# Slot scatters issued one by one, behind a unit's maxima and behind its norm

## The chip, the cores and the metric

The kernel runs on one core of a Trainium2 chip. The metric is the device time of one execution in microseconds (us). TensorE (PE in the rows, PEld for its weight loads), VectorE (DVE), ScalarE (ACT), GpSimd (POOL) and SyncE (SP) run their own instruction streams and meet at semaphores. A row that says "<-remote" tells of a wait whose releaser the profile cannot name.

## The reference

Pooled attention feeds a mixture of experts with one expert per token. Cut to what matters:

```python
k_p = k.reshape(B, H, S // 8, 8, D).mean(axis=3)          # B, H, S, D = 8, 8, 576, 64
v_p = v.reshape(B, H, S // 8, 8, D).mean(axis=3)
scores = q @ k_p^T / sqrt(D)
attn = exp(scores - max) / sum(exp(scores - max))
x = (attn @ v_p) as 4608 tokens of 512
e = argmax(x @ w_gate)                                     # 8 experts, hidden size 1024
pos = running count of e, token by token                   # dropped beyond capacity 1152
y = relu(x @ w1[e]) @ w2[e];  out = softmax(x @ w_gate)[e] * y
```

All numbers are float32; the products of the expert part are made of three products of a high and a low part each.

## The kernel before

**Two parts.** The attention part (from L388 on) makes the 4608 token rows, writes them to `xs` in HBM, and finds for each token its place in a table `slots` in HBM that is sorted by expert. The expert part (L1297 on) is a loop over items of up to 256 tokens of one expert; it gathers rows of `xs` by the table, makes the two products, and scatters rows to the output. Between them stands `prologue` (L1008), which reads the table back (L1041, L1042) after the last scatter into it and does the first item.

**Units.** The attention part walks over 36 units of 128 tokens (L707), in pairs of batches: four units of the even batch, a tail unit made of the last 64 tokens of both (`Unit.tail`, its matmuls work on 64 rows at a time), four units of the odd batch. The loop at L1148 is a software pipeline written out by hand: its turn n makes the scores of unit n (L499), their maxima (`softmax`, L506: `mx`) and the subtraction (L511), the exponential of unit n-1 (L514), and of unit n-2 the transposes of the probabilities (L523, copied by ScalarE at L524), the product with the values (`av`, L535: `pa`) and `norm` (L546 to L554: `rz` is the reciprocal of the sums, `xo` the result). The order in the loop is the order on each engine; nothing is moved by a scheduler.

**Queues of small work.** Work that is no part of a unit waits in lists: `rq` (routing, generators of small VectorE instructions), `gq` (GpSimd's sums of keys and values, later the splitting of expert weights), `aq`, `dq`, and `sq` (the slot scatters). `step(list, n)` at fixed places of the turn takes n pieces from a list and so fixes where they stand.

**Routing and slot scatters.** When the 9 (later 4, 2 and 3) logit groups of a batch pair are there, `route` (L586) works out on VectorE for each token its slot (`gix`, L684) and its gate weight (`pairs`, L688). Then it puts one scatter per group of 128 tokens into `sq` (L702), 27 for the first three pairs and 9 for the last. A scatter (L690) is two GpSimd instructions: a copy of one column into `apart`, which reads the tile that `pace` names, and the indirect DMA (L696) that writes 128 entries of 8 bytes to `slots`. `pace` is set in `softmax` to the unit's maxima (L508), so that the copy, and with it the scatter, waits until VectorE has made them. In the last two turns, where no unit is scored, `pace` is empty and a memset (L695) stands for the copy.

Before the change the scatters of a turn stand together at its end (L1228): two in a turn up to turn 25, four from turn 26. At turn 28 `start_ids` (L845) issues what is left in `sq` and then SP's load of the first slots (L848); the gather of their rows follows on GpSimd (L97) among pieces of `w1l` (L128), and its rows are transposed at turns 31 and 32 (L884). At turn 25 SP loads weights (L843), at turn 33 more of them (L124). ScalarE issues the writes of token rows to `xs` (L582).

Of the kernel before, what the change touches and what calls it, by code (L numbers as in the profile page):

```python
# [10 lines left out]
F32 = mybir.dt.float32  # L11
# [10 lines left out]
P = 128  # L22
# [9 lines left out]
def pooled_attn_top1_moe(ctx: ExitStack, tc: tile.TileContext, q, k, v, wg, w1, w2, cap, out):  # L32
# [8 lines left out]
    B, H, S, D = q.shape  # L41
# [126 lines left out]
    with ExitStack() as actx:  # L168
# [3 lines left out]
        sm = actx.enter_context(tc.tile_pool(name="sm", bufs=2))  # L172
# [188 lines left out]
        def tail_tile(b):  # L361
            return (b // 2) * NPB + (2 * NB if b < LAST - 1 else NB + 2)
# [112 lines left out]
        class Unit:  # L475
# [65 lines left out]
            def norm(self):  # L541

                b, t = self.b, self.t
                av = self.pa.rearrange("p (h x) -> p h x", x=XW)
                rz = sm.tile([P, H, 1], F32, name="rz", tag="rz")
                nc.vector.tensor_scalar_add(rz, av[:, :, XW - 1 : XW], POOL * 1e-9)  # L546
                nc.vector.reciprocal(rz, rz)
                i = 0 if self.tail else t % 2
                if i == 0:
                    self.xo = wk.tile([P, 1 if self.tail else 2, H, XW - 1], F32, name="xo", tag="xt" if self.tail else "xo", bufs=1 if self.tail else 3)  # L550
                    first[b, t] = self.xo
                else:
                    self.xo = first[b, t - 1]
                nc.vector.tensor_mul(self.xo[:, i], av[:, :, 0 : XW - 1], rz.to_broadcast([P, H, XW - 1]))  # L554
                if not self.tail and i == 0:
                    return
                bp = b // 2
                if bp not in lgs:
                    lgs[bp] = sm.tile([P, NPB, E], F32, name="lg", tag="lg")
                if self.tail:  # L560
                    t0 = tail_tile(b) - bp * NPB
                elif b == LAST:
                    t0 = NB + 3 * (t // 2)
                else:
                    t0 = (b % 2) * NB + t - 1
                nc.vector.tensor_reduce(out=lgs[bp][:, t0 : t0 + i + 1], in_=self.xo[:, :, :, D:].rearrange("p i h e -> p i e h"), axis=AX.X, op=ALU.add)
                if self.tail:
                    for u, bb in enumerate(self.bs):
                        rows_out.append((xs[bb * S + NB * P : (bb + 1) * S, :].rearrange("p (h d) -> p h d", d=D), self.xo[u * TAIL : (u + 1) * TAIL, 0, :, 0:D]))
                else:  # L570
                    if b == LAST:
                        r0 = b * S + P * (t - 1)
                        dst = xs[r0 : r0 + 2 * P, :].rearrange("(p j) d -> p j d", j=2)
                    else:
                        dst = xs[b * S : b * S + NB * P, :].rearrange("(p j) d -> p j d", j=NB)[:, t - 1 : t + 1]
                    rows_out.append((dst.rearrange("p j (h d) -> p (j h) d", d=D), self.xo.rearrange("p j h x -> p (j h) x")[:, :, 0:D]))
# [128 lines left out]
        pace = []  # L705
# [5 lines left out]
        rq, aq, dq, sq, gq, held, hold = [], [], [], [], [], [], [1]  # L711
# [32 lines left out]
        def step(q_, n=1):  # L744

            while q_ and n and not (q_ is rq and held):
                if callable(q_[0]):
                    q_.pop(0)()
                    n -= 1
                    continue  # L750
                made = next(q_[0], 0)
                if made == 0:
                    q_.pop(0)
                elif made is not held:
                    n -= 1
                elif hold:
                    held.append(1)
# [6 lines left out]
        with tc.manual_schedule():  # L764
# [20 lines left out]
            def ahead(b):  # L785

                if b + 1 < B:
                    load_q(b + 1)
                if b == LAST - 1:
                    dq.append(masks)  # L790

            nu = len(units)
# [3 lines left out]
            n_late = n_early + 6  # L796
# [39 lines left out]
            def start_early():  # L836

                drain(rq)
                e0 = nc.values_load(esi[0:1, 0:1], engines=(SP,), min_val=0, max_val=E - 1)
                early["e0"] = e0  # L840
                early["w1"] = [kv_tile()[:, 0:2].rearrange("p f x -> p (f x)") for _ in range(KD)]
                for c in range(KD):
                    nc.sync.dma_start(early["w1"][c], rows(w1f, e0 * DM + c * P, P))  # L843
# [12 lines left out]
            def start_weights():  # L856
                drain(gq)
                kvx.close()
                wb = ctx.enter_context(tc.tile_pool(name="wb", bufs=1, side="right", reuse_waits="tile"))
                wr[1] = wb.tile([P, KD, DF], F32, name="r1")  # L860
                wr[2] = wb.tile([P, KF, DM], F32, name="r2")
                wr["h"] = wb.tile([P, KF, DM], F32R, name="w2h")
                wr["l"] = wb.tile([P, KF, DM], F32R, name="w2l")
                load_w2(early["e0"])
# [5 lines left out]
            def split_next():  # L870
                for c in range(2):
                    for f in range(0, DM, 256):
                        gq.append(partial(w2_piece, c, slice(f, f + 256), nc.gpsimd))
# [274 lines left out]
            for n in range(nu + 2):  # L1148
                u = units[n] if n < nu else None
                if u is None:  # L1150
                    pace.clear()
                p = units[n - 2] if n > 1 else None
                nx = units[n + 1] if n + 1 < nu else None
                new = n and u and u.b != units[n - 1].b
                if new:
                    assert not aq
                    ahead(u.b)
                if n == nu:
                    hold.clear()
                if n == n_start:  # L1160
                    start_weights()
                if n == n_start + 2:
                    split_next()
                if n == n_early:
                    start_early()
                if n == n_early + 3:
                    start_ids()
                    split_early()
                if n == n_early + 4:
                    start_rows()  # L1170
                if u:
                    u.score(0)
                if p and n <= nu:
                    p.p_t(0)
                if 0 < n <= nu:
                    units[n - 1].exp()
                fed = n > NB and nx and values_at(n)
                if fed:
                    nx.q_part()
                spread(n)  # L1180
                if u:
                    u.score(1)
                    if n == 0:
                        keys_first(1, kfirst)
                    u.softmax()
                step(aq)
                if p and n <= nu:
                    p.p_t(1)
                if n == nu:
                    sums()  # L1190
                if nx and not fed:
                    nx.q_part()
                if held:
                    held.clear()
                    step(rq)
                turns(n)
                flush()
                step(aq)
                if n == nu:
                    hidden(0, [0])  # L1200
                    units[n - 1].p_t(0)
                    units[n - 1].p_t(1)
                    step(gq, 4)
                if p:
                    p.open()
                    p.av(0)
                    p.av(1)
                if n == nu:
                    hidden(0, [1])
                if n >= n_late:  # L1210
                    step(rq, 7 if n < nu else 9 if n == nu else 2)
                step(dq)
                if p:
                    p.norm()
                if n_early + 6 <= n < n_early + 8:
                    transposed(n - n_early - 6, early["x"])
                if n < nu:
                    step(rq, 4 if n <= nu // 2 else 8 if n < n_late else 4)
                elif n == nu:
                    step(rq, 3)  # L1220
                r = p and route_of(p)
                if r:
                    rq.append(r)
                    if p.b == early_b - 1:
                        rq.append(favourite())
                hooks(n)
                step(gq, 4 if n < nu - 1 else 0)
                step(sq, 2 if n < nu - 10 else 4)  # L1228
                step(aq)
            flush()  # L1230
            prologue()
# [137 lines left out]
```

## Time and profile before

| | |
|---|---|
| time, median of 3 runs | 661.72 us (657.91 to 663.55) |
| the profiled execution's own time | 656.15 us |
| its span, first to last instruction | 654.5 us |
| PE busy | 607.1 us (93%) |
| PEld busy | 539.8 us (82%) |
| DVE busy | 339.2 us (52%) |
| POOL busy | 317.9 us (49%) |
| ACT busy | 223.6 us (34%) |
| mean granted TensorE clock | 0.979 |

Busy times are shares of one profiled execution. Ends of matmuls are modelled, so a busy TensorE need not be at its peak. A wait's releaser is inferred from semaphore events. The time of a GpSimd DMA row is that of the issue on the engine, not of the data's way to HBM.

### The profile page before, as it was taken

Reading aid. Unit: us, or ns where it says so; the run is one execution under the profiler, and the core shown is the slowest. Engines: PE = TensorE matmul, PEld = TensorE weight load, DVE = VectorE, ACT = ScalarE, POOL = GpSimd, SP = SyncE. Lnnn points to the kernel's source line nnn. Section 1 sums busy time; section 2 is a strip of 40 time slices with the busy share of each in tenths; the row PEclk is TensorE's granted clock in tenths of the full one; section 3 lists DMA queues with packets and bytes.
Section 4 is the critical chain, followed back from the end, with each engine's and each line's share of the span. In section 5 each row is a group of like instructions: output and inputs, shape, how many; then the busy total and the mean of one; then the engine's idle time right before and its main releaser. Section 6 shows DMA issues by size and latency. Waiting matters only on the chain. (4 is left out here: it accounts for less than half of the span.)

```text
span 654.5 us, 13915 instructions
## 1 busy us (share of the span) xinstructions
PE 607.1 (93%) x3966; PEld 539.8 (82%) x3967; DVE 339.2 (52%) x740; ACT 223.6 (34%) x414; POOL 317.9 (49%) x537
## 2 busy tenths in 40 slices
PE   2899979989779799999999999999999999999994
PEld 2789869878668588898989899888998889989983
DVE  4777867868767812246728642235432565222222
ACT  2465444546424111135517521115211473112111
POOL 7399979247645334215745413414444155431344
PEclk9999989999979899999999999999999999999997
DMA  9999996584622271107845652102721091110111
GB/s 314 301 255 334 310 264 121 118 242 98 177 46 54 73 300 64 32 32 238 298 159 178 248 204 64 64 20 77 263 64 56 12 316 31 64 42 22 64 48 65
DMA packets 103712, 93.79 MB, mean 143 GB/s; under 512 B 82820, under 2 KB 82820, under 8 KB 103688
## 3 DMA queue, kind: packets, MB, share of 16 engines
q1 hardware_dynamic: 54520, 62.47, 30.1%
q0 software_dynamic: 11392, 21.57, 10.4%
q10 hardware_dynamic: 37776, 9.46, 6.5%
q8 instruction: 12, 0.20, 0.1%
q14 instruction: 12, 0.10, 0.1%
HBM read 132.96 MB, written 31.27 MB: 251 GB/s over the span
## 5 line engine op out<-in xcount | busy, mean ns | idle before, releaser
L1269 DVE SCALAR_TENSOR_TENSOR hl<-ph,hh 128x512 fp32r<-128x512 f32 x60 | 40.8, 690 | 108.9 <-ACT hh L1268 78.0
L1268 ACT ACTIVATE hh<-ph 128x512 fp32r<-128x512 f32 x60 | 35.9, 599 | 171.2 <-PE ph L152 168.3
L165 PE MATMUL y<-w2h,hh 128*128 128x512 f32 x280 | 78.1, 400 | 0.0
L152 PE MATMUL ph<-xh,w1h 128*128 128x256 f32 x480 | 76.5, 281 | 1.2 <-ACT xo L1084 0.9
L165 PE MATMUL y<-w2l,hh 128*128 128x512 f32 x280 | 76.6, 395 | 0.0
L152 PE MATMUL ph<-xl,w1h 128*128 128x256 f32 x480 | 76.2, 280 | 0.4 <-DVE w1l L128 0.3
L152 PE MATMUL ph<-xh,w1l 128*128 128x256 f32 x480 | 76.0, 280 | 0.0
L97 POOL DMA_INDIRECT xg<-xs,ix x42 | 44.2, 1053 | 58.9 <-PE y L165 52.2
L165 PE MATMUL y<-w2h,hl 128*128 128x512 f32 x280 | 71.0, 396 | 0.0
L152 PEld LDWEIGHTS ph<-xh,w1h 128*128 128x128 f32 x480 | 65.7, 188 | 4.5 <-issue 1.9
L152 PEld LDWEIGHTS ph<-xl,w1h 128*128 128x128 f32 x480 | 65.0, 188 | 0.7 <-issue 0.7
L152 PEld LDWEIGHTS ph<-xh,w1l 128*128 128x128 f32 x480 | 65.0, 188 | 0.0
L165 PEld LDWEIGHTS y<-w2h,hl 128*128 128x128 f32 x280 | 52.6, 188 | 12.7
L165 PEld LDWEIGHTS y<-w2l,hh 128*128 128x128 f32 x280 | 52.6, 188 | 12.6
L535 PE MATMUL pa<-vbd,pT 126*128 126x146 f32 (+5 forms) x400 | 60.6, 313 | 0.0
L535 PEld LDWEIGHTS pa<-vbd,pT 126*128 126x128 f32 (+1 forms) x400 | 56.4, 184 | 3.0 <-issue 0.7
L165 PEld LDWEIGHTS y<-w2h,hh 128*128 128x128 f32 x280 | 50.0, 188 | 9.4
L524 ACT COPY pT<-pp 126x384 f32<-126x384 f32 x72 | 30.3, 422 | 78.6 <-PE pp L523 56.7
L128 DVE TENSOR_TENSOR xl<-px,xh 128x512 fp32r<-128x512 f32 x40 | 25.7, 686 | 57.2 <-ACT xh L127 57.2
L102 POOL DMA_INDIRECT out_dram<-zrow,iz x40 | 46.8, 1171 | 16.3 <-issue 15.1
L499 PE MATMUL ps<-kbs,qT 128*128 128x144 f32 (+1 forms) x320 | 52.9, 308 | 1.8 <-ACT qT L490 1.8
L95 POOL TENSOR_TENSOR guard<-ix 128x4 int32<-128x4 int32 x21 | 5.1, 244 | 101.6 <-DVE ix L92 101.3
(261 smaller groups left out, 1035.6 us busy)
## 6 DMA issues: line engine op xcount, KB each, us to landing
r<-in_moe_w_dram SPq DMA_DIRECT2D x86, 1024.0 KB
raw<-in_k_dram SPq DMA_DIRECT2D x12, 768.0 KB
raw<-in_v_dram SPq DMA_DIRECT2D x12, 768.0 KB
qblk<-in_q_dram SPq DMA_DIRECT2D x32, 256.0 KB
xs<-xo ACTq DMA_DIRECT2D x16, 512.0 KB
raw<-in_moe_w_dram SPq DMA_DIRECT2D x4, 512.0 KB
qtail<-in_q_dram SPq DMA_DIRECT2D x8, 128.0 KB
xs<-xo ACTq DMA_DIRECT2D x8, 128.0 KB
```

Of the source, the lines that this page charges most:

```text
L95: nc.gpsimd.tensor_sub(guard, ix, ix)
L97: nc.gpsimd.indirect_dma_start(out=dst[:, i, :].bitcast(F32), out_offset=None, in_=src, in_offset=bass.IndirectOffsetOnAxis(ap=ix[:, i, 0: ...
L102: ins = nc.gpsimd.indirect_dma_start(out=out[:, :], out_offset=bass.IndirectOffsetOnAxis(ap=i_, axis=0), in_=src, in_offset=None, bounds_c ...
L128: eng.tensor_sub(lo, src, hi.bitcast(F32))
L152: nc.tensor.matmul(p[:, f2], a[:, c, f * P : (f + 1) * P], b[:, c], start=(f2 == 0 and j == 0 and c == 0), stop=(f2 == 1 and j == 2 and c ...
L165: nc.tensor.matmul(y, a[:, c, i * P : (i + 1) * P], b[:, c], start=(first and n == 0), stop=(last and n == len(terms) - 1))
L499: nc.tensor.matmul(self.ps[us, h, 0 : 2 * SP_].rearrange("p (a x) -> p a x", a=2), self.qT[:, h, us], kbs[b // 2 % 2][:, :, b % 2, h], sta ...
L524: nc.scalar.copy(self.pT[:, cs.start : cs.stop], pp[0:KC, 0 : len(cs)])
L535: made = nc.tensor.matmul(self.pa[us, h0 * XW : (h0 + nh) * XW], self.pT[:, c, us], vbd[b % 2][:, c, 0:nh].rearrange("r s x -> r (s x)"), ...
L1268: nc.scalar.activation(hh[s], p, AF.Relu)
L1269: nc.vector.scalar_tensor_tensor(out=hl[s], in0=p, scalar=0.0, in1=hh[s].bitcast(F32), op0=ALU.max, op1=ALU.subtract)
```

## The change

`norm` now also sets `pace`, to the first column of its `rz`, as long as units are being scored; `rz` gets four buffers in place of two, as `mx` has. The scatters leave the end of the turn. One stands right behind `softmax`, and waits for this turn's maxima. Behind `norm` stands one more up to turn 30, two in turns 31 to 35, four in the last two turns; these wait for `rz` of the same turn. The work that a scatter does is the same, and there are 36 as before.

```diff
@@ -542,9 +542,11 @@
                 av = self.pa.rearrange("p (h x) -> p h x", x=XW)
-                rz = sm.tile([P, H, 1], F32, name="rz", tag="rz")
+                rz = sm.tile([P, H, 1], F32, name="rz", tag="rz", bufs=4)
                 nc.vector.tensor_scalar_add(rz, av[:, :, XW - 1 : XW], POOL * 1e-9)
                 nc.vector.reciprocal(rz, rz)
+                if pace:
+                    pace[:] = [rz[:, 0]]
@@ -1183,6 +1185,7 @@
                     u.softmax()
+                    step(sq)
                 step(aq)
@@ -1212,6 +1215,7 @@
                 if p:
                     p.norm()
+                step(sq, 1 if n < n_late else 2 if n < nu else 4)
                 if n_early + 6 <= n < n_early + 8:
@@ -1225,7 +1229,6 @@
                 step(gq, 4 if n < nu - 1 else 0)
-                step(sq, 2 if n < nu - 10 else 4)
                 step(aq)
```

Here `nu` is 36, `n_early` 25 and `n_late` 31. On TensorE, VectorE, ScalarE and SyncE the instructions stand in the same order as before; only GpSimd's order changes, and what some instructions wait for. VectorE's first instruction of `norm` (L546) gets a wait for the GpSimd copy that read its buffer four turns earlier, as the maxima (L506) had for theirs.

The first place is GpSimd at the second batch pair, whose slots are ready at the end of turn 23. `mx` and `rz` carry a number per turn: 1574 is the maxima of turn 23, 1638 those of turn 24, 1721 of turn 25. Before, with the second scatter of each turn and its copy left out:

```order
L693 COPY apart_165<-mx_1574 128x1
L696 DMA slots_65<-pairs_67,gix_1560 36864x2
...
L693 COPY apart_165<-mx_1638 128x1
...
L693 COPY apart_165<-mx_1721 128x1
...
L693 COPY apart_165<-mx_1780 128x1
```

Two scatters name each of 1574, 1638 and 1721, three name 1780 (turn 26). In the changed kernel 1634 is the maxima of turn 24, 1672 the norm of turn 24, and so on to 1815 and 1843 of turn 27:

```order
L695 COPY apart_165<-mx_1634 128x1
L698 DMA slots_65<-pairs_67,gix_1560 36864x2
L695 COPY apart_165<-rz_1672 128x1
...
L695 COPY apart_165<-mx_1717 128x1
...
L695 COPY apart_165<-rz_1741 128x1
...
L695 COPY apart_165<-mx_1815 128x1
...
L695 COPY apart_165<-rz_1843 128x1
```

The nine scatters start a turn later and each has a release of its own, but for the last two, which both wait for the norm of turn 27; the last of them now stands in turn 28, in front of SP's load of the slots.

The second place is GpSimd at the third batch pair, whose slots are ready at turn 31, behind the splits of `w1l`. Before, 2042 is the maxima of turn 31 (four scatters), 2130 of turn 32 (four), 2192 of turn 33 (one), 2257 of turn 34 (the four of the next group):

```order
L128 TENSOR_TENSOR w1l_86<-raw_1704,w1h_85 128x256 x4
L693 COPY apart_165<-mx_2042 128x1
...
L693 COPY apart_165<-mx_2130 128x1
...
L693 COPY apart_165<-mx_2192 128x1
...
L693 COPY apart_165<-mx_2257 128x1
...
L128 TENSOR_TENSOR w2l_2177<-r2_2175,w2h_2176 128x256 x4
L695 MEMSET apart_165 128x1
```

In the changed kernel 2122 and 2144 are turn 32, 2182 and 2226 turn 33, 2251 and 2297 turn 34, 2319 and 2334 turn 35; each `mx` releases one scatter and each `rz` two:

```order
L128 TENSOR_TENSOR w1l_86<-raw_1700,w1h_85 128x256 x4
L695 COPY apart_165<-mx_2122 128x1
...
L695 COPY apart_165<-rz_2144 128x1
...
L695 COPY apart_165<-mx_2182 128x1
...
L695 COPY apart_165<-rz_2226 128x1
...
L695 COPY apart_165<-mx_2251 128x1
...
L128 TENSOR_TENSOR w2l_2167<-r2_2165,w2h_2166 128x256 x4
L697 MEMSET apart_165 128x1
```

The fifth scatter of the nine moved from behind the maxima of turn 32 to behind the norm of turn 33, and one scatter moved behind the splits of `w2l`, where six stand now and five stood.

## Rows read from the trace of the kernel before

**Rows 1.** The page: the span.

```profile
span 654.5 us, 13915 instructions
```

**Rows 2.** Stretches: length, busy us of each engine, granted clock, DMA share, GB/s.

```profile
0.00:88.00 88.00, 72.00 (x533) 64.42 (x534) 62.59 (x129) 43.40 (x103) 70.54 (x150) 1.00 1.02 301
88.00:213.00 125.00, 107.80 (x786) 98.43 (x784) 92.75 (x304) 55.89 (x132) 73.39 (x117) 0.95 0.56 133
...
233.00:654.50 421.50, 411.53 (x2586) 365.12 (x2584) 169.84 (x261) 121.51 (x176) 165.62 (x263) 0.99 0.33 114
```

**Rows 3.** Waits of the whole trace: who for whom, total us, times, longest.

```profile
ACT pT L524 <- remote: 12.2, 2, 8.9
...
PE pq L489 <- ACT pT L524: 9.5, 3, 7.0
...
DVE rz L546 <- remote: 8.7, 2, 5.1
```

**Rows 4.** All engines in order of time, turn 24: start, us, what, idle before.

```profile
131.97 0.73 PE L535 MATMUL pa<-vbd,pT 126*64 126x219 f32 x10
...
134.26 0.98 POOL L696 DMA_INDIRECT slots<-pairs,gix  x1 [0.16 <-issue]
...
136.11 0.17 DVE L546 TENSOR_SCALAR rz<-pa 128x8 f32<-128x8 f32 x1 [3.63 <-remote]
...
136.71 0.44 PE L489 MATMUL pq<-identr,qblk 128*128 128x128 f32 x2 [2.28 <-ACT pT L524]
```

**Rows 5.** All engines in order of time, turn 33.

```profile
181.29 0.17 DVE L546 TENSOR_SCALAR rz<-pa 128x8 f32<-128x8 f32 x1 [5.07 <-remote]
...
181.91 0.98 POOL L696 DMA_INDIRECT slots<-pairs,gix  x1 [0.16 <-issue]
...
184.25 0.48 ACT L524 COPY pT<-pp 126x384 f32<-126x384 f32 x1 [8.89 <-remote]
...
184.78 0.47 PE L489 MATMUL pq<-identr,qblk 128*128 128x128 f32 x1 [6.98 <-ACT pT L524]
```

**Rows 6.** Stretches: behind the second wait; and around five scatters, twice.

```profile
184.70:189.20 4.50, 4.42 (x18) 4.31 (x19) 2.58 (x13) 1.59 (x5) 0.18 (x1) 0.50 0.29 58
...
110.00:118.50 8.50, 8.50 (x68) 7.77 (x67) 7.83 (x24) 3.77 (x8) 7.52 (x13) 1.00 0.59 129
...
205.00:212.00 7.00, 5.84 (x46) 5.50 (x46) 5.63 (x26) 3.20 (x7) 5.41 (x10) 1.00 0.15 31
```

**Rows 7.** GpSimd in order of time: scatters, slot gather and splits.

```profile
127.08 0.18 POOL L693 COPY apart<-mx 128x1 f32<-128x1 f32 x1 [8.66 <-DVE gse L686]
...
130.23 0.98 POOL L696 DMA_INDIRECT slots<-pairs,gix  x1 [2.97 <-DVE fw L805]
...
147.99 0.98 POOL L696 DMA_INDIRECT slots<-pairs,gix  x1 [0.16 <-issue]
...
155.03 1.00 POOL L97 DMA_INDIRECT xg<-xs,idp  x1 [0.16 <-issue]
...
168.02 2.80 POOL L128 TENSOR_TENSOR w1l<-raw,w1h 128x256 fp32r<-128x256 f32 x4 [5.03 <-ACT w1h L127]
...
171.11 1.02 POOL L696 DMA_INDIRECT slots<-pairs,gix  x1 [0.17 <-issue]
...
205.36 0.98 POOL L696 DMA_INDIRECT slots<-pairs,gix  x1 [4.47 <-DVE pairs L688]
```

**Rows 8.** VectorE and TensorE in order of time: maxima, norm, transposes of gathered rows.

```profile
130.94 0.76 DVE L506 TENSOR_REDUCE mx<-ps 128x8 f32<-128x576 f32 x1
...
149.02 0.16 DVE L546 TENSOR_SCALAR rz<-pa 128x8 f32<-128x8 f32 x1
...
166.50 0.51 PE L884 MATMUL pxe<-identr,xg 128*128 128x128 f32 x4
...
171.40 0.17 DVE L546 TENSOR_SCALAR rz<-pa 128x8 f32<-128x8 f32 x1 [0.21 <-PE pa L535]
...
173.54 0.75 DVE L506 TENSOR_REDUCE mx<-ps 128x8 f32<-128x576 f32 x1
```

## The prediction

> **What bounds the kernel now.** I read the page for the span [rows 1], then the stretches. The expert loop from 233 us on holds 421.5 of the 654.5 us and TensorE is busy for 411.5 of them [rows 2]; the change touches nothing there. In the stretch of 88 to 213 us, where all 36 slot scatters lie, TensorE is busy for 107.8 of 125.0 us at a mean clock of 0.95 [rows 2]. So 17 us of idle time and the clock are what a change of the scatters can win, and the end of this stretch moves the loop one for one, since the loop follows it on the same engine.
>
> The waits of the whole trace tell where these microseconds go. TensorE waits 9.5 us for ScalarE's copy of the transposed probabilities (L524) in three places, and that copy itself waits 12.2 us, and the norm 8.7 us, in two places each, for something that the profile cannot name [rows 3]. In order of time these are turns 24 and 33. In turn 24 the norm starts at 136.11 after 3.63 us, and TensorE's next transposes at 136.71 after 2.28 us of idle time [rows 4]. In turn 33 the norm starts at 181.29 after 5.07, the copy at 184.25 after 8.89, TensorE at 184.78 after 6.98 us, and from there to 189.20 its clock is 0.50 [rows 5, 6], the lower of its two levels (1.2 of 2.4 GHz). I call both a hold: the product with the values has been issued (at 131.97 in turn 24 [rows 4]), and what waits for it is released late.
>
> What the two holds have in common: GpSimd issues scatters back to back. The slots of the second pair are ready late in turn 23; two scatters of that turn and two of turn 24 go at once, the first at 130.23, the last at 134.26, ending at 135.24; the norm is released 0.87 us later [rows 4, 7]. In turn 33 nine run from 171.11 to 181.91 + 0.98 = 182.89, and the copy is released 1.36 us later [rows 5, 7]; they are (181.91 - 171.11) / 8 = 1.35 us apart, which is the engine's own pace, so no copy into `apart` held any of them up. Both turns also take the product of a tail unit, 64 rows at a time (for turn 24 [rows 4]). Two groups of five scatters pass without a hold: in 110.0 to 118.5 TensorE is busy for all 8.50 us, in 205 to 212 at full clock [rows 6]. So a train goes with the holds, but does not make one everywhere.
>
> **The change part by part.** Number and kind of the instructions stay: 36 scatters and their copies. What moves:
>
> *Second pair, turns 23 to 28.* The scatters of turn 23 go. The first now waits for the maxima of turn 24, ready at 130.94 + 0.76 = 131.70 [rows 8]; the second for the norm of turn 24. So one scatter is under way at the product of turn 24, where three stood in front of 134.26. If the train makes the hold, this one ends about 131.70 + 0.35 + 0.98 = 133.0 (0.35 is what the copy and its gap take, 1.35 less 0.98), a release 0.87 us behind it is at 133.9, and no more than normal waiting is left: TensorE gets its 2.28 us back. If it doesn't, the gain is nothing. I take 2.3.
>
> *Third pair, turns 31 to 34.* Nothing goes in turn 31, but GpSimd is at `w1l` until 170.8 anyway (168.02 + 2.80) [rows 7]. Then the first scatter is free (maxima of turn 32), the second and third follow the norm of turn 32 (171.40 + 0.17 and a reciprocal, about 171.8), the fourth the maxima of turn 33 (173.54 + 0.75 = 174.29) [rows 8]. At 1.35 us each, four run back to back from 171.1 to about 176.2, as before. The fifth waits for the norm of turn 33, which is what was held: the train ends at four instead of nine. A release 1.36 us behind 176.2 would be 177.6 instead of 184.25. What the hold costs is 6.98 us of idle TensorE and, behind it, 4.42 us of work at half the clock, which full clock does in 2.2 [rows 5, 6]: 9.2 us. The bounds are nothing (four scatters in front of the tail unit's product are enough, as four were in turn 24) and 9.2 (no hold). I take the middle, 4.6: four were enough there, but the release should come with the end of the train.
>
> *Last scatter of the second pair.* It moves from turn 26 (147.99) to turn 28, behind the norm of turn 27 at 149.02 + 0.16 and a reciprocal about as long, so from 149.4 or so: with 1.35 it ends near 150.8 instead of 148.97, 1.8 us later [rows 7, 8]. Behind it on GpSimd stand `w1l` and the gather of the first rows, on SP the load of the first slots. The gather goes from 155.03 to at most 156.9; its rows are needed at 166.50 [rows 7, 8], some 9 us later. The last pieces of `w1l` wait 5.03 us for ScalarE before 168.02 [rows 7], so a delay of 1.8 ends there. Price: nothing; without this cover 1.8 us.
>
> *First pair, turns 16 to 20.* Pieces of the sums of keys and values move behind at most two scatters, 2.7 us. GpSimd then idles 8.66 us before 127.08 [rows 7], and the sums are first read in turn 23, so this costs nothing.
>
> *One scatter behind the splits of `w2l`.* GpSimd waits 4.47 us there for the last slots, until 205.36 [rows 7]; one more scatter takes 1.35. Nothing.
>
> *VectorE's new wait in the norm*, for a GpSimd copy of four turns before: GpSimd would have to be four turns late, and in the trace it is late by two (the scatters of turns 31 and 32 at turn 33). Nothing.
>
> Sum: -2.3 - 4.6 = -6.9 us. The profiled execution took 656.15 us, 1.65 more than its span; it would take 649.3. It stands 5.6 us below the median of the three runs, which is the time to be compared with: 661.72 - 6.9 = 654.8 us.
>
> **The rivals.**
>
> *The trains do not make the holds; nothing changes.* For it: the two groups of five without a hold [rows 6], and that the holds fall on tail units, which the change leaves. The Trainium skill, page "SBUF — State Buffer", section "Who interferes with whom", says that TensorE and ScalarE never wait on any other engine's access and that a DMA never contends with a compute engine; by it neither a scatter nor its issue could hold TensorE's product. The full 8.50 us in 110.0 to 118.5 agree with it; the two holds, which no engine of the profile releases, are what it does not explain. The time is then 661.7 us. A half of this rival: only turn 24 is freed, four scatters hold turn 33 as long as nine, and the time is 661.72 - 2.3 = 659.4.
>
> *Each scatter beside a product can hold it, and now more turns have one; slower.* Its place is turns 33 to 35, where each turn now issues three scatters of which two wait for the norm. If the fifth, behind the norm of turn 33, runs into the product of turn 34, that turn is held as well, and the last group does the same in turn 35. One more hold of the size of turn 33 costs 9.2 us: 661.72 + 9.2 = 670.9. It decides from the point at which one or two scatters are enough for a hold. Against it: before, too, scatters stood in many turns between 88 and 213 us, and the profile shows only two holds [rows 3].
>
> **How the numbers follow.** Forecast, both holds shrink (half of the second, or all): 0.43. The rival with no change 0.28, its half 0.16, the slower one 0.13. A measurement of this kernel can tell a change of about 1% from none; 1% of 661.72 us is 6.6, so the borders are 655.1 and 668.3. Faster by over 1%: the forecast, 0.43 (650.2 to 654.8; what of it misses the border is about made up by spread of the other cases). Within 1%: 0.28 + 0.16 = 0.44. Slower: 0.13. The range for 8 in 10 takes in both bounds of the gain, 661.72 - 2.3 - 9.2 = 650.2 and 661.7, and half of the spread of the three runs (2.8) on either side, rounded: 647 to 664. It leaves out the slower rival. The likeliest case alone is 650 to 656.
>
> **What would show it.** In the changed kernel's waits the unnamed releases of the norm and of the copy fall from 8.7 and 12.2 us to below 4 each; TensorE's clock in 182 to 190 us stays at 1.00; in turn 24 one scatter stands between the maxima and the norm; in turn 33 four scatters run, then GpSimd waits for the norm. If the step on turn 33 is wrong, the copy is released again 5 us or more behind the product although only four scatters went before. If the step on the cover is wrong, the transposes of gathered rows (L884) show a wait for their DMA. The prediction fails if the unnamed waits stay as long as they are, or if they turn up in other turns than 24 and 33.

## The result, and the profile of the changed kernel

The changed kernel takes 652.98 us (median of 20 runs), the kernel before, run beside it, 659.95 us (20 runs, 657.91 to 663.55). The ratio is 0.988, with a 95% interval of 0.986 to 0.990. Three of the changed kernel's 20 runs (659.54, 659.87 and 2056.68 us) are slow ones, which the ratio leaves out and the median keeps. The ratios of this text are not quotients of the medians, from which they differ by up to 0.005. The forecast was 654.8 us in 647 to 664. The profiled execution of the changed kernel:

```profile
span 653.6 us, 13931 instructions
```

That is only 0.9 us shorter than the span before [rows 1], for a reason that comes below. The windows of the stretch with all scatters, of the expert loop and of the place of the second hold, with the busy time of each engine, TensorE's granted clock, the DMA share and GB/s:

```profile
core 0: us, PE busy (x) PEld busy (x) DVE busy (x) ACT busy (x) POOL busy (x), PEclk, DMA share, GB/s
88.00:213.00 125.00, 112.80 (x828) 102.67 (x826) 94.51 (x310) 58.72 (x136) 76.82 (x121) 0.95 0.59 137
233.00:653.60 420.60, 410.69 (x2582) 364.28 (x2580) 170.02 (x261) 121.37 (x176) 166.10 (x261) 1.00 0.32 111
...
182.00:190.00 8.00, 7.32 (x57) 7.10 (x57) 7.12 (x26) 2.67 (x7) 6.29 (x13) 1.00 0.44 93
```

The expert loop is as long as it was, 410.7 us of TensorE where 411.5 stood [rows 2]. In 88 to 213 us TensorE is busy for 112.8 us, 5.0 more than before (42 more matmuls fall into the window), and in 182 to 190 its clock is 1.00, where the stretch behind the second hold had 0.50 [rows 6]. From the waits of the whole trace (engine and line, what was waited for, total, times, longest):

```profile
POOL apart L695 <- DVE mx L506: 22.0, 5, 9.2
DVE rz L546 <- PE pa L535: 18.6, 20, 3.1
...
PE pxe L886 <- DMA xg<-xs,idp: 3.4, 2, 2.4
...
POOL apart L695 <- DVE rz L547: 3.0, 3, 1.4
...
DVE rz L546 <- PE ps L152: 2.4, 1, 2.4
```

The unnamed releases of ScalarE's copy (12.2 us) and of the norm (8.7 us) [rows 3] are gone; the norm now waits for its own product, L535. GpSimd waits longer in their place, which is what the change built: 22.0 us for the maxima, where it waited 9.5 before, and 3.0 us for the norm, a wait that is new. One more line is new and matters below: the norm waits 2.4 us and the profile names L152, a matmul that has nothing to do with it. The timeline of turn 33, tail unit's product first (start, duration, engine, line):

```profile
177.14 1.60 PE L535 MATMUL pa<-vbd,pT 126*64 126x146 f32 x20
...
178.04 0.98 POOL L698 DMA_INDIRECT slots<-pairs,gix  x1 [0.16 <-issue]
179.89 0.17 DVE L546 TENSOR_SCALAR rz<-pa 128x8 f32<-128x8 f32 x1 [1.01 <-PE pp L523]
180.02 0.48 ACT L524 COPY pT<-pp 126x384 f32<-126x384 f32 x1 [2.13 <-PE pp L523]
180.09 0.20 DVE L547 RECIPROCAL rz<-rz 128x8 f32<-128x8 f32 x1
180.43 0.18 POOL L695 COPY apart<-rz 128x1 f32<-128x1 f32 x1 [1.40 <-DVE rz L547]
180.56 0.66 PE L489 MATMUL pq<-identr,qblk 128*128 128x128 f32 x4
181.11 0.98 POOL L698 DMA_INDIRECT slots<-pairs,gix  x1 [0.50 <-issue]
```

The scatter at 178.04 is the fourth of its row; the fifth waits 1.40 us for the norm, as forecast. TensorE goes on at 180.56 without a wait, where it stood idle for 6.98 us before [rows 5].

A table of turns shows where the time went. It gives the time from the start of one turn's maxima (L506) to that of another, and from the maxima of turn 35 to the norm (L546) of turn 37, from the timelines of each kernel. The second pair of columns is from a later profile of the same two kernels (before_again and after_again, below), the third is from a chip on which no turn is held (loads_later, whose order is the one of before, and after_third, below).

| us | before | after | before, chip 13 | after, chip 13 | before's order, chip 7 | after, chip 7 |
|---|---|---|---|---|---|---|
| turn 24 to 25 | 7.59 | 4.43 | 6.79 | 4.43 | 4.31 | 4.43 |
| turn 33 to 34 | 10.71 | 5.36 | 10.50 | 5.49 | 4.21 | 4.27 |
| turn 24 to 35 | 60.23 | 49.51 | 57.72 | 49.45 | 47.51 | 48.31 |
| turn 35 to norm 37 | 10.03 | 12.70 | 9.61 | 12.95 | 9.62 | 9.75 |

The change takes 10.7 us out of turns 24 to 35 and gives 2.7 back behind turn 35: 8.0 net, where the ratio says 0.012 x 660 = 7.9; on chip 13 it is 8.3 less 3.3, 4.9 net, where the ratio found there (0.9936) says 4.2. That the two profiled spans differ by 0.9 only lies outside of these turns: the maxima of turn 24 begin at 136.35 in the changed kernel, at 130.94 before [rows 8], 5.4 us later, and from the norm of turn 37 to the end it takes 455.0 us where 453.3 stood, 1.7 more (8.0 - 5.4 - 1.7 = 0.9). The runs below show that the start varies from run to run; the end does too, from 453.3 to 456.0 us over the six profiles of the table.

### The profile page after: what moved, and what is told of

It reads as the page before. It is cut to its first block, busy times and chain, and to the rows that moved or that the text cites. A ratio compares the mean times of both kernels' runs of the same rounds, so it can differ in the third digit from the quotient of the medians.

```text
span 653.6 us, 13931 instructions
## 1 busy us (share of the span) xinstructions
PE 609.6 (93%) x3966; PEld 542.9 (83%) x3967; DVE 336.9 (52%) x740; ACT 223.6 (34%) x414; POOL 320.0 (49%) x537
## 5 line engine op out<-in xcount | busy, mean ns | idle before, releaser
L152 PE MATMUL ph<-xh,w1h 128*128 128x256 f32 x480 | 77.2, 283 | 1.2 <-ACT xo L1086 0.9
L152 PE MATMUL ph<-xl,w1h 128*128 128x256 f32 x480 | 76.5, 281 | 0.4 <-DVE w1l L128 0.2
L152 PE MATMUL ph<-xh,w1l 128*128 128x256 f32 x480 | 76.7, 282 | 0.0
L152 PEld LDWEIGHTS ph<-xh,w1h 128*128 128x128 f32 x480 | 66.4, 190 | 4.4 <-issue 2.0
L152 PEld LDWEIGHTS ph<-xl,w1h 128*128 128x128 f32 x480 | 65.4, 190 | 0.7 <-issue 0.7
L152 PEld LDWEIGHTS ph<-xh,w1l 128*128 128x128 f32 x480 | 65.7, 191 | 0.0
L165 PEld LDWEIGHTS y<-w2h,hl 128*128 128x128 f32 x280 | 52.6, 188 | 12.7
L165 PEld LDWEIGHTS y<-w2l,hh 128*128 128x128 f32 x280 | 52.6, 188 | 12.7
L535 PE MATMUL pa<-vbd,pT 126*128 126x146 f32 (+5 forms) x400 | 61.6, 317 | 0.9 <-DVE pairs L690 0.7
L535 PEld LDWEIGHTS pa<-vbd,pT 126*128 126x128 f32 (+1 forms) x400 | 57.6, 187 | 3.5 <-ACT pt L514 0.9
```

Of the source, the lines that this page charges most:

```text
L152: nc.tensor.matmul(p[:, f2], a[:, c, f * P : (f + 1) * P], b[:, c], start=(f2 == 0 and j == 0 and c == 0), stop=(f2 == 1 and j == 2 and c ...
L165: nc.tensor.matmul(y, a[:, c, i * P : (i + 1) * P], b[:, c], start=(first and n == 0), stop=(last and n == len(terms) - 1))
L535: made = nc.tensor.matmul(self.pa[us, h0 * XW : (h0 + nh) * XW], self.pT[:, c, us], vbd[b % 2][:, c, 0:nh].rearrange("r s x -> r (s x)"), ...
```

## Experiments

The theory to be tested was the prediction's: scatters back to back beside a tail unit's product hold its release, and the change breaks the rows of scatters. The rivals were that the holds have another cause, and that it is the place, or the wait for the norm, that counts.

### Half of the change at a time, the trains elsewhere, and the wait for the norm alone

Four kernels on one chip (number 7). The first has the change up to turn 29 only, the second from turn 30 on only:

```diff
-                if pace:
+                if pace and b < 6:
                     pace[:] = [rz[:, 0]]
...
                     u.softmax()
-                    step(sq)
+                    if n < 30:
+                        step(sq)
...
-                step(sq, 1 if n < n_late else 2 if n < nu else 4)
+                if n < 30:
+                    step(sq)
...
                 step(gq, 4 if n < nu - 1 else 0)
+                if n >= 30:
+                    step(sq, 4)
```

(this is early_half, against the changed kernel; late_half has the conditions the other way round).

> The change up to turn 29 (first and second pair), the kernel before from turn 30 on (third and fourth pair). Trains make the holds: turn 24 runs without a hold (no unnamed release of the norm or the copy above 1 us there), turn 33 keeps its own (unnamed releases of the copy and the norm of 5 us or more, clock 0.50 behind it); of the 7.0 us between the kernels (659.95 and 652.98) it gets some 2, so about 658. No connection between trains and holds: holds come and go by chance, in either turn, and the time lies anywhere between 653 and 660 without a hold to go with it.

> The kernel before up to turn 29, the change from turn 30 on. Trains make the holds: turn 24 keeps its hold (3 to 4 us of unnamed release, 2 to 3 us of idle TensorE), turn 33 has none; of the 7.0 us it gets some 5, so about 655. No connection: as in the run of the other half, and the two gains do not add up to 7. That the place, not the number, of the scatters counts is not told apart by this run.

The third is the kernel before with other numbers of scatters at the turns' ends; the fourth is the changed kernel without the two lines that make the norm set the pace:

```diff
-                step(sq, 2 if n < nu - 10 else 4)
+                step(sq, {23: 0, 24: 0, 25: 5, 26: 5, 31: 0, 32: 0, 33: 0, 34: 7, 35: 6}.get(n, 2 if n < nu - 10 else 4))
```

> The kernel before, with its scatters at the turn's end, but none in the turns 23, 24 and 31 to 33: the second pair's go as five in turn 25 and four in turn 26, the third pair's in turns 34 and 35 with the fourth pair's first ones. Trains are as long as before or longer, but none stands beside a tail unit's product. If a train needs a tail unit's product to make a hold: no unnamed release in any turn, about 653 as in the changed kernel. If a train alone makes a hold: unnamed releases of 3 us or more in turns 25, 26, 35 or 36, and about 660 as before. If the holds have nothing to do with scatters: unnamed releases in turns 24 and 33 as before, though no scatter stands there, about 660.

> The changed kernel with every scatter's copy released by the latest maxima, also the ones behind a norm. The program's order is the changed one; only the wait for the norm is gone. If it is the wait for the norm that breaks the train of turn 33: the scatters run seven in a row from about 173 to 183 us, the hold of turn 33 is back with 4 us or more, about 657 to 658. If the place in the order does it: no hold, about 653.

| kernel | us, median | ratio to the kernel before, 95% |
|---|---|---|
| the kernel before, beside them | 648.49 | |
| early_half | 647.35 | 1.0008 (0.9978 to 1.0039) |
| late_half | 649.26 | 1.0016 (0.9995 to 1.0036) |
| trains_moved | 648.23 | 0.9983 (0.9947 to 1.0020) |
| pace_max | 647.88 | 0.9981 (0.9946 to 1.0016) |

None of the expectations was met in its numbers, because the kernel before itself took 648.49 us here, 11.5 us less than in the first comparison. No kernel of the four has an unnamed release of the norm or of the copy. early_half still has the trains of before in turns 31 to 34, and in its profile they run thirteen in a row, from 167.92 to 185.08 us; its turn 33 to 34 takes 4.24 us. A train of scatters beside a tail unit's product is therefore not enough for a hold. late_half shows how far a single profile can stray without one: its turns 24 to 35 take 50.26 us, 2.75 more than the 47.51 of the table, with TensorE's clock at 0.82 from 165 to 170 us and at 0.84 from there to 175. What had to be known next was whether the holds belong to the kernel or to the chip.

### The same two kernels again, and one longer train

On chip 13, the kernel before and the changed kernel without an edit, and the kernel before with all nine scatters of the second pair at the end of turn 23:

```diff
-                step(sq, 2 if n < nu - 10 else 4)
+                step(sq, {23: 9}.get(n, 2 if n < nu - 10 else 4))
```

> The kernel before, unchanged, profiled once more, since its median beside the four runs so far is 648.5 us and no longer 660. Holds belong to the kernel: unnamed releases of the copy and the norm of 3 us or more in turns 24 and 33 again, and TensorE idle there for 2 and 7 us. Holds belong to some chips or moments only: the trains stand as before in turns 24 and 33 (four and nine scatters, 1.35 us apart), no unnamed release above 1 us, TensorE busy for over 18 of 20 us in 130 to 150 and in 170 to 190, and a span near 647.

> The changed kernel, unchanged, beside the kernel before on the same chip. If the change's gain is nothing but the two holds, and this chip has none in the kernel before (648.5): a ratio of 1.00, within 0.995 and 1.005. If the change gains also without holds: 0.988, some 641. If it loses elsewhere what the holds hid (its profiled execution was 5.4 us behind at the maxima of turn 23): up to 1.008, some 654; then the loss shows between 88 and 110 us.

> The kernel before with all nine scatters of the second pair at the end of turn 23, so that some twelve us of back-to-back scatters stand beside the tail unit's product of turn 24. If a train beside a tail unit's product makes a hold on any chip: an unnamed release in turn 24 of 5 us or more, TensorE idle for as long, 5 us or more above the kernel before beside it. If trains do not make holds by themselves: TensorE busy for over 18 of 20 us in 130 to 150, a ratio of 1.00.

Here the kernel before took 657.58 us (23 runs) and the copy of it 658.53 (ratio 1.0017, 0.9983 to 1.0052). The changed kernel took 651.00 (0.9936, 0.9907 to 0.9965), the kernel with the long train 665.60 (four runs; 1.0168, 1.0109 to 1.0227). The holds are back in the kernel before, in the same two turns. Turn 33 of its timeline:

```profile
175.67 1.60 PE L535 MATMUL pa<-vbd,pT 126*64 126x146 f32 x20
...
180.42 0.98 POOL L696 DMA_INDIRECT slots<-pairs,gix  x1 [0.16 <-issue]
180.88 0.17 DVE L546 TENSOR_SCALAR rz<-pa 128x8 f32<-128x8 f32 x1 [3.46 <-remote]
...
181.76 0.98 POOL L696 DMA_INDIRECT slots<-pairs,gix  x1 [0.16 <-issue]
...
183.10 0.98 POOL L696 DMA_INDIRECT slots<-pairs,gix  x1 [0.16 <-issue]
183.83 0.48 ACT L524 COPY pT<-pp 126x384 f32<-126x384 f32 x1 [7.38 <-remote]
...
184.36 1.12 PE L489 MATMUL pq<-identr,qblk 128*128 128x128 f32 x4 [5.37 <-issue]
```

TensorE is idle for 5.37 us. The norm is let go at 180.88, with two scatters of the row still to come, and the copy at 183.83, while the last one runs (to 184.08). So the release does not wait for the end of the train; that it stood 0.87 and 1.36 us behind it in the first trace [rows 4, 5, 7] was chance. The long train says the same. Its turns 24 and 25:

```profile
133.11 1.60 PE L535 MATMUL pa<-vbd,pT 126*64 126x146 f32 x20
...
137.28 0.17 DVE L546 TENSOR_SCALAR rz<-pa 128x8 f32<-128x8 f32 x1 [2.79 <-PE pp L523]
...
138.73 0.48 ACT L524 COPY pT<-pp 126x384 f32<-126x384 f32 x1 [3.87 <-remote]
...
139.26 1.12 PE L489 MATMUL pq<-identr,qblk 128*128 128x128 f32 x4 [2.83 <-issue]
...
142.25 0.37 ACT L524 COPY pT<-pp 126x256 f32<-126x256 f32 x1 [2.46 <-remote]
...
143.00 0.98 POOL L696 DMA_INDIRECT slots<-pairs,gix  x1 [0.16 <-issue]
```

The hold of turn 24 is only 0.7 us longer than in the kernel before beside it (TensorE idle for 2.83 us, there 2.15), though the row has nine scatters in place of four. What the longer train adds is a second unnamed wait, of 2.46 us in turn 25, which has no tail unit, and the clock behind it (windows with the columns of the first section):

```profile
133.00:137.50 4.50, 3.44 (x35) 2.83 (x33) 1.67 (x6) 1.85 (x4) 3.95 (x8) 1.00 0.69 160
137.50:141.00 3.50, 1.74 (x7) 1.74 (x8) 2.40 (x11) 1.06 (x2) 3.05 (x5) 0.65 1.03 364
141.00:146.00 5.00, 4.12 (x15) 3.25 (x14) 2.09 (x5) 0.96 (x2) 2.65 (x5) 0.50 0.52 171
146.00:152.00 6.00, 6.00 (x26) 5.48 (x25) 2.77 (x7) 1.91 (x4) 0.00 (x0) 0.50 0.88 186
```

TensorE works at half its clock (1.2 of 2.4 GHz) from 141 to 152 us, busy for 10.1 of 11.0 us. What that costs can be read from one product: ten matmuls of L535 take 1.58 us at the full clock, and 3.12 in the kernel before on this chip, behind the hold of turn 33, at 0.50. From turn 24 to 26 this kernel needs 17.91 us, the one before beside it 12.00: 5.9 of the 8.0 us that it is slower. On this chip, then, scatters do make holds: a longer row of them makes more, and the changed kernel, with its row broken, has at most 1.2 us of one left in these turns (turn 33). A tail unit's product is not needed.

The profile of the changed kernel, in both of its executions on chips with holds, shows that a third one has come into being. From turn 33 on GpSimd has three scatters a turn, 3 x 1.35 = 4.05 us of a turn of some 4.3, so that the row closes up again, and eight run from 181.11 to 192.23 us. Turn 36 of the first profile of the changed kernel:

```profile
189.91 0.98 POOL L698 DMA_INDIRECT slots<-pairs,gix  x1 [0.16 <-issue]
190.01 1.58 PE L535 MATMUL pa<-vbd,pT 126*128 126x146 f32 x10
191.25 0.98 POOL L698 DMA_INDIRECT slots<-pairs,gix  x1 [0.16 <-issue]
...
193.30 0.17 DVE L546 TENSOR_SCALAR rz<-pa 128x8 f32<-128x8 f32 x1 [2.41 <-PE ps L152]
...
194.55 0.39 PE L650 MATMUL pa<-su,upper 128*128 128x8 f32 x2 [1.50 <-DVE xo L556]
...
195.41 3.04 PE L535 MATMUL pa<-vbd,pT 126*128 126x146 f32 x10
```

and its windows, as above:

```profile
186.00:190.00 4.00, 4.00 (x32) 4.00 (x33) 3.44 (x9) 1.42 (x4) 3.50 (x7) 1.00 0.01 1
190.00:191.60 1.60, 1.60 (x13) 1.60 (x12) 0.81 (x8) 0.00 (x0) 1.44 (x3) 1.00 0.90 201
...
194.00:199.00 5.00, 4.45 (x20) 4.29 (x21) 2.33 (x9) 0.83 (x4) 3.79 (x7) 0.66 0.01 2
```

The product of turn 36 ends at 190.01 + 1.58 = 191.59, the norm comes at 193.30, TensorE is idle for 1.50 us, and the next product takes 3.04 us where 1.58 is usual, the clock being 0.66 in the window of 194 to 199. These are the 2.7 (and on chip 13 3.3) us of the table that are given back.

The same turn of the first trace of the kernel before has the same product behind four scatters:

```profile
195.13 0.98 POOL L696 DMA_INDIRECT slots<-pairs,gix  x1 [0.16 <-issue]
195.22 1.58 PE L535 MATMUL pa<-vbd,pT 126*128 126x146 f32 x10
...
197.03 0.17 DVE L546 TENSOR_SCALAR rz<-pa 128x8 f32<-128x8 f32 x1 [0.93 <-PE pa L535]
```

```profile
195.20:197.10 1.90, 1.90 (x16) 1.90 (x15) 0.88 (x9) 0.17 (x1) 0.91 (x1) 1.00 0.91 202
```

The DMA engines are as busy beside it (share 0.91, 202 GB/s) as beside the product of the changed kernel (0.90, 201 GB/s), and the norm comes 0.23 us behind the product's end, where the row of eight has 1.71. So the transfer alone does not make the hold. The row alone does not seem to either: the product of turn 35 stands in the same row of eight, ends at 187.66 us, with the DMA share at 0.01 from 186 on, and its norm comes at 187.70. Every hold in the traces begins where the DMA share is 0.7 or more, and no run took the transfer away, so a row of scatters together with a transfer is a rival to the row alone that stands untested.

### The changed kernel on a chip without holds, and three more tries

The next four ran on chip 7 again: the changed kernel, trains_moved and pace_max once more, and the kernel before with its weight loads written one turn later.

```diff
-                if n == n_start:
+                if n == n_start + 1:
                     start_weights()
...
-                    start_early()
+                    drain(rq)
+                if n == n_early + 1:
+                    start_early()
```

> The changed kernel once more, for the question whether its gain hangs on the chip. Where the kernel before beside it takes some 657 to 660 us (a chip with holds): ratio 0.988 to 0.994 as in the two comparisons so far. Where it takes some 648 (a chip without holds): ratio 1.00, within 0.995 and 1.005, since the changed kernel has nothing to win there. If the gain does not hang on the holds: 0.99 on such a chip too, some 642.

> The kernel before with its trains moved out of the turns of the tail units: five scatters in turn 25, four in 26, seven in 34, six in 35, none in 23, 24 and 31 to 33. On a chip with holds: if a train needs a tail unit's product, no unnamed release above 1 us and a ratio of 0.99 (651); if a train alone is enough, unnamed releases of 3 us or more in turns 25, 26, 34 or 35 and a ratio of 1.00; if the scatters are not what holds, holds in turns 24 and 33 as before, 1.00. On a chip without holds: 1.00 and no unnamed release, as in its first run.

> The kernel before with its scatters as they are, and the weight loads that start in turns 24 to 25 and 33 (first layer of the first expert's weights, L843, and second layer, L124) issued one turn later. On a chip with holds: if the train by itself holds, turns 24 and 33 keep unnamed releases of 3 us or more, ratio 1.00; if it takes a train and a load together, these releases fall below 1 us in both turns and stand a turn later if anywhere, ratio 0.99. On a chip without holds: 1.00 and nothing to tell.

> The changed kernel's order with every copy released by the latest maxima. On a chip with holds: if the wait for the norm of turn 33 is what breaks the train, seven scatters go in a row there and the hold of turn 33 is back with 4 us or more, ratio 1.00; if the order of the code is enough, ratio 0.99 and no unnamed release above 1 us. On a chip without holds: 1.00, as in its first run.

| kernel | us, median | ratio to the kernel before, 95% |
|---|---|---|
| the kernel before, beside them | 647.70 | |
| after_third (the changed kernel) | 649.02 | 1.0014 (0.9983 to 1.0045) |
| trains_moved_2 | 647.68 | 1.0000 (0.9975 to 1.0024) |
| loads_later | 647.69 | 1.0004 (0.9966 to 1.0042) |
| pace_max_2 | 648.83 | 0.9986 (0.9956 to 1.0016) |

On this chip the change is worth nothing: the interval leaves out any gain of more than 0.2%. The new hold is not there either; turn 36 of the changed kernel on this chip has its norm right behind the product, at the end of a row of eight scatters as dense as the one above and beside a transfer (DMA share 0.90 from 189.0 to 190.7 us):

```profile
189.04 1.58 PE L535 MATMUL pa<-vbd,pT 126*128 126x146 f32 x10
...
190.73 0.17 DVE L546 TENSOR_SCALAR rz<-pa 128x8 f32<-128x8 f32 x1 [0.78 <-PE pa L535]
...
192.84 1.68 PE L535 MATMUL pa<-vbd,pT 126*128 126x146 f32 x10
```

loads_later did not do what it was made for. SyncE issues these loads when their own waits end, wherever the code has them: 0.93 us behind the start of the maxima of turn 24 (133.07 and 132.14) and 1.14 us behind those of turn 32 (168.49 and 167.35), where the kernel before has them too (1.35 us behind the maxima of turn 24, 132.29 and 130.94 [rows 8]). So whether a load has to stand beside the train for a hold was not tried by a run. But the kernel is the one before in all that counts here, and its profile is the counterpart to turn 33 of before [rows 5] on a chip without holds:

```profile
172.12 1.60 PE L535 MATMUL pa<-vbd,pT 126*64 126x146 f32 x20
...
172.84 0.98 POOL L696 DMA_INDIRECT slots<-pairs,gix  x1 [0.16 <-issue]
173.79 0.15 DVE L546 TENSOR_SCALAR rz<-pa 128x8 f32<-128x8 f32 x1
174.18 0.98 POOL L696 DMA_INDIRECT slots<-pairs,gix  x1 [0.16 <-issue]
174.82 0.48 ACT L524 COPY pT<-pp 126x384 f32<-126x384 f32 x1 [1.96 <-PE pp L523]
175.35 0.66 PE L489 MATMUL pq<-identr,qblk 128*128 128x128 f32 x4
```

Scatters stand beside the product, 1.34 us apart, and the norm comes at 173.79, 0.07 us behind the product's end (172.12 + 1.60). Its thirteen scatters run from 168.75 to 185.91.

The last run was meant for a chip with holds and got one without (number 5, the kernel before at 648.37 us):

> The kernel before with its trains moved, a third time, for a chip on which the kernel before has holds (some 655 to 660 us beside it). There, if scatters beside a tail unit's product make the holds: none in any turn, a ratio of 0.985 to 0.993, and the maxima of turn 35 some 52 to 54 us behind those of turn 23. If a train alone makes a hold: unnamed releases of 3 us or more in turns 25, 26, 34 or 35, a ratio of 0.995 to 1.005. If scatters have nothing to do with it: the same in turns 24 and 33. On a chip without holds (some 648 beside it): 1.00 and 52 us, as twice before, and the question stays open.

It took 645.89 us, a ratio of 0.9963 (0.9933 to 0.9994; the interval leaves out 1, but the same kernel had 0.9983 and 1.0000 on chip 7), with no unnamed release and 47.74 us from turn 24 to 35, as in its other two profiles (47.56, 47.75). So whether a train far from tail units, or the order without the wait for the norm, is held on a chip with holds was not seen. No version tried is shown to be faster than the changed kernel where there are holds, or clearly faster than the kernel before where there are none.

## Why the prediction came out as it did

The number was right for the chip on which it was measured: 654.8 forecast, 652.98 measured, a gain of 6.9 us forecast and 7.0 measured between the medians (7.9 by the ratio). It was counted from 661.72 us, the median of three runs; from the 659.95 of the 20 runs the same sum gives 653.05. The steps under it held less well.

*The two holds as the thing to win*: right where there are holds. From turn 24 to 35 the kernel before needs 60.23 and 57.72 us on such chips and 47.51 on one without: the holds cost 12.7 and 10.2 us there, and account for the 9 to 12 us between the kernel's medians (657.58 and 659.95, and 647.70 to 648.49). That they depend on the chip was not in the prediction at all. It read one trace as if it were the kernel's nature; on chip 7 there was nothing to win.

*Turn 24, -2.3 us*: the first comparison gives 7.59 - 4.43 = -3.2, the second 6.79 - 4.43 = -2.4. What is left is the 4.43 that the changed kernel also needs on the chip without holds, so no part of the hold is left.

*Turn 33, -4.6 us*: the mis-sized term. Turn 33 to 34 fell by 5.3 and 5.0 us, and with the half-clock stretch behind it (turn 34 to 35, 6.92 to 4.30 and 5.51 to 4.29) by 8.0 and 6.2. The working took the middle between nothing and 9.2, because four scatters go before the wait and the release was thought to come with the train's end. Four scatters in front of this product held it by 1.1 and 1.2 us only (5.36 and 5.49 against 4.27), and the release does not come with the end of the train, as turn 33 of the copy and the long train showed.

*No price anywhere else*: failed by 2.7 to 3.3 us. This is the slower rival's mechanism: in turns 33 to 35 each turn issues three scatters, two of them behind the norm, and this piles up eight in a row. The rival saw a whole hold of 9.2 us in turn 34 or 35; it came in turn 36 and cost a third of that. The prediction had named late releases in other turns than 24 and 33 as a sign of its failing, and this one, which the profile puts down to L152, is such a sign. By chance the gain that was taken too small in turn 33 and the loss that was left out nearly cancel: the sum was right by luck, for reasons that are half right.

*The cover of the last scatter of the second pair*: held. The gather now starts 10.5 us in front of the transposes of its rows (158.68 and 169.17), where it was 11.5 (155.03 and 166.50 [rows 7, 8]), and they do not wait for it. The 3.4 us that L886 waits for gathered rows belong to a second gather behind turn 37 (at 221.98 and 223.50 us), and the kernel before has 3.4 us there in its first trace too.

*The first pair, nothing*: not refuted, though the changed kernel's first trace seems to speak against it (turn 24 begins 5.4 us late there). In early_half, with the changed order of the first two pairs, turn 24 begins at 131.35 us, in late_half, with the order of before, at 135.12; over the eight profiles with the first pair's order of before it lies between 130.94 and 135.12 (mean 132.95), over the six with the changed one between 131.35 and 136.57 (mean 134.75). Most of the 5.4 us is a start that varies from run to run; a cost of up to the 1.8 us between the means is not excluded, and chip 7, where the changed kernel is 1.3 us above the kernel before (interval -1.1 to +2.9), does not exclude it either.

*The wait behind the splits of `w2l` and VectorE's new wait, nothing*: no row of either trace speaks against them; no run tried them alone.

*No connection between trains and holds*: this rival is refuted on the chip with holds by the long train (1.0168, a hold in a turn that had none) and by the changed kernel, whose hold moved with its scatters. On chip 7 it describes what happens: 1.0014. What the prediction brought for it is less than it seems, since the five scatters of 110.0 to 118.5 us are no row: 1.6 us of GpSimd's sums stand between the second and the third. The Trainium skill, page "SBUF — State Buffer", section "Who interferes with whom", says that TensorE and ScalarE wait on no other engine's access and that DMA does not contend with compute. Thirteen scatters in a row without a hold on chip 7 agree with it; the holds on the other chips are not explained by it.

What is open: what it is on a chip with holds that keeps a release back, so that those who need it wait 2.4 to 8.9 us. The runs show that there a longer row of scatters makes a hold where a shorter one makes none (turn 25 of the long train, turn 36 of the changed kernel), and that neither the end of the row nor a tail unit's product is what decides. Whether a transfer has to stand beside the row, as one does at the start of every hold seen, is open too.

## What to carry to other kernels

An unnamed wait that is long, and twice the same, may still belong to the chip on which the trace was taken: profile the kernel before a second time on another chip before a change is sized by it. When a change spreads work over more turns to break one row, look whether what it puts into a turn still leaves the turn a gap; here three scatters fill 4.05 of some 4.3 us, and the new row of eight gave back 2.7 of 10.7 us and 3.3 of 8.3. And a sum that comes out right is no proof of its terms; the turn-by-turn table showed two errors that cancelled.

## What the runs showed of the hardware that was not expected

The same program took 648.49, 647.70 and 648.37 us on chips 7, 7 and 5, and 659.95 and 657.58 us in the first comparison (whose chip is not on record) and on chip 13. By the table of turns a few late releases of TensorE's results, with the stretches at half clock behind them, account for the whole difference (12.7 and 10.2 us). The traces of the two sorts of chip differ in one more thing. From the DMA issues of the copy of the kernel before (chip 13), and of loads_later (chip 7), the last number being the median time from issue to landing:

```profile
slots<-pairs,gix POOLq DMA_INDIRECT x36
```

```profile
slots<-pairs,gix POOLq DMA_INDIRECT x36, 4.4
```

On chip 13 the profile has no landing time for these scatters, on chip 7 it has one, 4.4 us. It is not the scatters only: of 21 kinds of DMA issues each of the five traces with holds has a landing time for one, and the nine traces without holds have it for 13 to 18. Whether the missing records and the late releases have one cause was not tried, and the runs do not tell. Each of them has a recorded span and clock, so none shows what the kernel takes when nothing is recorded.
